# Spreading one row of a table over all SBUF partitions: through DRAM on SyncE's queue, or in one transfer from one partition on GpSimd's queue

## The chip, the cores and the metric

The kernel runs on one core of one Trainium2 chip. The metric is the device time of one execution in microseconds. TensorE (PE) multiplies matrices, VectorE (DVE) and ScalarE (ACT) do elementwise work, GpSimd (POOL) does small copies and issues transfers, and SyncE (SP) issues transfers only. Each engine takes its own list of instructions in order.

## The reference, cut to what matters

```python
def reference(x, w_in, w_out):               # x: 8 x 3008 x 256, d_ff = 2048
    X = np.fft.fft(np.fft.fft(x, axis=1), axis=2).real      # mixing
    t = X.reshape(24064, 256)
    h = np.maximum(t @ w_in, 0.0)
    return h * h @ w_out                     # 24064 x 256
```

The two transforms are matrix products with cosine and sine tables. The real part of the two-dimensional transform is a sum of a cosine product and a sine product. Output rows k and S - k (S = 3008) share both products: one is their sum, the other their difference. The transform over the 256 features is folded into the first weight, so that the first product of the second stage works on the half spectrum, d = 0 to 128.

## The kernel before, in words

The work is cut into 25 windows (`wins`) of up to 512 pairs of output rows; the loop `for w in range(NW)` takes them in order. For every window there are two f16 tiles of 128 partitions, `zc` (cosine part) and `zs` (sine part), four buffers each. They are made ahead: during window w, `z_steps` fills the columns of window w + 1 with matmuls into `pz` (line 536), an ACT copy (line 545) and, for the mirrored columns, a DVE operation on `zs` and `zc` (line 552). These jobs are spread over the steps `lo` to `hi` of a window.

A window has eight steps, `s0` = 0 to 7, each of two chunks of 128 columns of the first weight. In an ordinary step PE multiplies `gh` with `zc` and `zs` into `ph` (lines 804 and 805), ACT takes the relu (line 814), PE turns the sign of the sine part by a third matmul (line 810), and ACT and DVE square both results into `h2` (lines 817 and 819). In the steps that `plan(w)` lists in groups of one or two, the mirrored half is made on DVE instead: PE multiplies the sine part (line 829), ACT copies it times -2 into `sn` (line 837), PE adds the cosine part (line 843), ACT copies it into `hd` (line 845), and DVE adds the two (line 867), takes the relu (line 868) and squares (line 869).

The partition of `zs` that would belong to d = 0 of the sine part is zero in itself and holds the cosine part's row for d = 128 instead. In the mirrored half its sign must not turn, so `sn` has to be corrected: for every chunk a DVE instruction multiplies that row, `eb`, spread over all 128 partitions, by a number per partition, `wv` (line 853, two per step of a group), and another adds it to `sn` (line 857). `row_spread(w)` makes `eb[w]`: it first copies partition 0 of `zs` into a row `zr` in DRAM (line 643), and then reads that row into all 128 partitions (line 645). The second half is kept in the list `row_back` and issued at the head of step 7. `row_spread(w + 1)` is called behind step `hi - 1` of window w (5 in most windows, 6 in some; behind the two steps of a pair where steps go by twos), and only for windows that have groups. `eb` has two buffers. There are 22 such windows.

The second product, `ffn2_steps`, belongs to the window before: PE multiplies `h2` with `wout16` into `po` (line 683), 16 matmuls a piece, ACT copies `po` to `osb` (line 698; three buffers), and `store` issues one or several transfers to the output on SyncE's queue (line 662). These pieces are spread over the eight steps of the next window, so the SyncE list holds stores and the row's two transfers in the order of the program.

For each of the eight batches DVE folds the input (`fold_steps`): `fe`, `fo`, `ab`, `od` and `ev` on lines 392 to 422, with the last value of `od` out of a small matmul (line 418). GpSimd's list holds the loads of `x` (lines 133 and 138, some of them by row indices), the store of `ev` to a DRAM scratch `scr` (line 424), its loads back into `rb` (lines 432 and 434), and four small copies per batch (lines 464 to 466).

Of the kernel before, what the change touches and what calls it, by code (L numbers as in the profile page):

```python
# [9 lines left out]
F16 = mybir.dt.float16  # L10
# [5 lines left out]
P = 128  # L16
# [12 lines left out]
def kernel(  # L29
# [14 lines left out]
    nc = tc.nc  # L44
# [10 lines left out]
    WN = 512  # L55
# [61 lines left out]
    drp = ctx.enter_context(tc.tile_pool(name="drp", bufs=2, space=bass.MemoryType.DRAM))  # L117
# [392 lines left out]
    def zwin(w):  # L510
        if w not in zc:
            zc[w] = zp.tile([P, WN], F16, name="zc", tag="zc")
            zs[w] = zp.tile([P, WN], F16, name="zs", tag="zs")
        return zc[w], zs[w]
# [67 lines left out]
    def run(*jobs):  # L582
        for j in jobs:
            j()
# [48 lines left out]
        nc.vector.tensor_scalar(out=wv, in0=pv[:, 0:NFC], scalar1=2.0, scalar2=None, op0=ALU.mult)  # L633

    eb = {}
    row_back = []

    def row_spread(w):

        wn = wins[w][1]  # L640
        t = eb[w] = tmp.tile([P, WN], F16, name="eb", tag="kf")
        zr = drp.tile([1, WN], F16, name="zr", tag="zr")
        nc.sync.dma_start(out=zr[0:1, 0:wn], in_=zwin(w)[1][0:1, 0:wn])
        src = zr[0:1, 0:wn]
        row_back.append(lambda: nc.sync.dma_start(out=t[:, 0:wn], in_=bass.AP(tensor=src.tensor, offset=src.offset, ap=[[0, P], [1, wn]])))

    def store(osb, p0, g0, m, minus, eng=nc.sync):

# [79 lines left out]
    NST = NFC // 2  # L728
# [16 lines left out]
    def halved(w):  # L745

        return plan(w)[0]
# [4 lines left out]
    for w in range(NW):  # L752
        g0, wn = wins[w]
# [46 lines left out]
        def pq(s):  # L800
            ph = phs[s] = ps_h.tile([P, 2, 512], F32, name="ph", tag="psh")
            for a in range(2):
                f0 = (2 * s + a) * P
                nc.tensor.matmul(ph[:, a, 0:wn], gh[:, 0, f0 : f0 + P], zcw[:, 0:wn], start=True, stop=False)  # L804
                nc.tensor.matmul(ph[:, a, 0:wn], gh[:, 1, f0 : f0 + P], zsw[:, 0:wn], start=False, stop=True)  # L805

        def turn(s):
            for a in range(2):
                f0 = (2 * s + a) * P
                nc.tensor.matmul(phs[s][:, a, 0:wn], gh[:, 2, f0 : f0 + P], zsw[:, 0:wn], start=False, stop=True, skip_group_check=True)  # L810

        def square(s, sg):
            h1 = h1p.tile([P, 2, 512], F16, name="h1", tag="h1")
            nc.scalar.activation(h1[:, :, 0:wn], phs[s][:, :, 0:wn], AF.Relu)  # L814
            hv = rev_dim(h1[:, :, 0:wn], 2) if sg else h1[:, :, 0:wn]
            if sg == 0 and s in by_act:
                nc.scalar.activation(h2[:, 2 * s : 2 * s + 2, 0:wn], hv, AF.Square)  # L817
                return []
            return [lambda: nc.vector.tensor_tensor(h2[:, 2 * s : 2 * s + 2, sg * wn : (sg + 1) * wn], hv, hv, op=ALU.mult)]  # L819
# [5 lines left out]
        def half_q(s):  # L825
            ph = phs[s] = ps_h.tile([P, 2, 512], F32, name="ph", tag="psh")
            for a in range(2):
                f0 = (2 * s + a) * P
                nc.tensor.matmul(ph[:, a, 0:wn], gh[:, 1, f0 : f0 + P], zsw[:, 0:wn], start=True, stop=True)  # L829
            g = two[s]  # L830
            if s == g[0]:
                i = ROT[0] % 2
                ROT[0] += 1
                sns[g] = const.tile([P, 2 * len(g), WN], F16, name=f"sn{i}", tag=f"w16_{i}")
                hds[g] = tmp.tile([P, 2 * len(g), 2 * WN], F16, name="hd", tag="tt")
            i = 2 * g.index(s)
            nc.scalar.activation(sns[g][:, i : i + 2, 0:wn], ph[:, :, 0:wn], AF.Copy, bias=0.0, scale=-2.0)  # L837

        def half_p(s):
            ph, g = phs[s], two[s]  # L840
            for a in range(2):
                f0 = (2 * s + a) * P
                nc.tensor.matmul(ph[:, a, 0:wn], gh[:, 0, f0 : f0 + P], zcw[:, 0:wn], start=False, stop=True, skip_group_check=True)  # L843
            i = 2 * g.index(s)
            nc.scalar.activation(hds[g][:, i : i + 2, 0:wn], ph[:, :, 0:wn], AF.Copy, bias=0.0, scale=1.0)  # L845

        def row_sum(s):

            g = two[s]
            sn, hd = sns[g][:, :, 0:wn], hds[g][:, :, wn : 2 * wn]  # L850

            def row(a):
                nc.vector.tensor_scalar(out=hd[:, a, :], in0=eb[w][:, 0:wn], scalar1=wv[:, 2 * g[0] + a : 2 * g[0] + a + 1], scalar2=None, op0=ALU.mult)  # L853

            if s < g[-1]:
                return []
            return [lambda a=a: row(a) for a in range(2 * len(g))] + [lambda: nc.vector.tensor_tensor(sn, sn, hd, op=ALU.add)]  # L857

        def halves(s):

            if s not in two or s != two[s][-1]:
                return []
            g = two[s]
            sn, hd = sns[g], hds[g]
            hv = hd[:, :, 0 : 2 * wn]
            return [
                lambda: nc.vector.tensor_tensor(rev_dim(hd[:, :, wn : 2 * wn], 2), hd[:, :, 0:wn], sn[:, :, 0:wn], op=ALU.add),  # L867
                lambda: nc.vector.tensor_scalar(out=hv, in0=hv, scalar1=0.0, scalar2=None, op0=ALU.max),  # L868
                lambda: nc.vector.tensor_tensor(h2[:, 2 * g[0] : 2 * g[-1] + 2, 0 : 2 * wn], hv, hv, op=ALU.mult),  # L869
            ]  # L870

        def others(s):
            for j in at[s]:
                j()
            for j in spread(f2, s, NST):
                j()
            for j in post[s]:
                j()
            if s == lo:
                zl[:] = [j for zu, part, h in zj for j in zu(part, h)]  # L880
            if s >= lo:
                for j in spread(zl, s - lo, hi - lo) if s < hi else []:
                    j()
# [44 lines left out]
        for s0 in range(0, NST, ng):  # L928
            ss = range(s0, s0 + ng)
            left = halves(s0 - 1)  # L930
            if s0 == NST - 1:
                while row_back:
                    row_back.pop()()
            if s0 in two and ng == 2:
                for s in ss:
                    half_q(s)
                others(s0)
                run(*row_sum(s0 + 1))
                for s in ss:
                    half_p(s)  # L940
                others(s0 + 1)
                continue
            if s0 in two:
                half_q(s0)
                rows = row_sum(s0)
                run(*(left[0:1] + rows[0:1] + left[1:2] + rows[1:-1] + left[2:3] + rows[-1:]))
                others(s0)
                half_p(s0)
                if s0 == hi - 1 and w + 1 < NW and halved(w + 1):
                    row_spread(w + 1)  # L950
                continue
            for s in ss:
                pq(s)
            for s in ss:
                run(*(left[0:2] + square(s, 0) + left[2:3]))
                left = []
            others(s0)
            for s in ss:
                turn(s)
            for s in ss:  # L960
                run(*square(s, 1))
            if s0 == hi - 1 and ng == 1 and w + 1 < NW and halved(w + 1):
                row_spread(w + 1)
            for s in ss[1:]:
                others(s)
            if s0 < hi <= s0 + ng - 1 and w + 1 < NW and halved(w + 1):
                row_spread(w + 1)
        while row_back:
            row_back.pop()()
        old = (w, h2)  # L970
    for j in ffn2_steps(*old, tail=True):
        j()
# [30 lines left out]
```

## Time and profile before

| | |
|---|---|
| median of 3 runs | 604.29 us (603.27 to 604.42) |
| the profiled execution, its own time | 603.7 us |
| its span, first to last instruction | 601.7 us |
| granted TensorE clock | 0.999 |
| busy: PE, weight loads, DVE, ACT, GpSimd | 579.0, 420.0, 512.5, 514.1, 84.3 us |
| chain of work that ended last | PE 59%, DVE 17%, ACT 10%, DMA 5%, SyncE 1% of the span |

The profile is of one execution. A line of the groups or of a timeline gives the source line, the engine, the operation, the tile written and the tiles read, the shape, and the busy time; the idle time in front of an instruction is named with what ended it. A busy PE is not a PE at its peak, since its matmuls are pipelined and their ends modelled. Idle time of an engine that no other waits for costs nothing.

### The profile page before, as it was taken

The numbers are of one execution on the slowest core, as the hardware profiler recorded it, in microseconds if no ns is written. First come the engines' busy times: TensorE is split into PE (matmuls) and PEld (weight loads), VectorE is DVE, ScalarE is ACT, GpSimd is POOL, SyncE is SP. The second block draws the span as 40 slices with busy tenths as digits, with TensorE's granted clock in tenths as the row PEclk, the third lists the DMA queues.
The fourth block names the chain that finished last, engine by engine and source line by source line (L and its number), as shares of the span: only waits on it lengthen the run. The fifth ranks groups of instructions, "written<-read, shape, count | busy, mean of one in ns | idle before, by whom it ended". The sixth has DMA issues, their size and how long they took to land.

```text
span 601.7 us, 11384 instructions
## 1 busy us (share of the span) xinstructions
PE 579.0 (96%) x4376; PEld 420.0 (70%) x4376; DVE 512.5 (85%) x747; ACT 514.1 (85%) x661; POOL 84.3 (14%) x130
## 2 busy tenths in 40 slices
PE   5899999999999999999999999999999899999997
PEld 2557776776777677777777777777677676776786
DVE  7897578887999987989889899887996899889981
ACT  7687787889999889989999898988989788888972
POOL 6360201102002032020011200411000110000000
PEclk9999999999999999999999999999999999999999
DMA  8955311273224524441164212633112231121222
GB/s 146 203 111 134 90 41 44 46 155 96 64 51 88 135 89 93 107 127 46 53 123 108 87 47 55 113 87 111 49 32 74 69 93 36 46 59 45 64 59 68
DMA packets 39737, 50.33 MB, mean 84 GB/s; under 512 B 4589, under 2 KB 33539, under 8 KB 39683
## 3 DMA queue, kind: packets, MB, share of 16 engines
q0 software_dynamic: 9344, 22.14, 18.3%
q1 hardware_dynamic: 30111, 27.26, 16.0%
q8 instruction: 34, 0.56, 0.4%
q10 hardware_dynamic: 228, 0.21, 0.1%
q14 instruction: 20, 0.16, 0.1%
HBM read 36.42 MB, written 27.86 MB: 107 GB/s over the span
## 4 chain that ended last, share of the span: by engine, by line
PE 59%; DVE 17%; ACT 10%; issue 6%; DMA 5%; SPq 1%; POOL 0%; DVEq 0%; ACTq 0%; POOLq 0%
PE po L683 35%; PE ph L843 5%; PE ph L810 4%; PE ph L829 4%; PE ph L804 4%; PE ph L805 4%; DVE h L869 3%; ACT h L814 3%; PE pz L536 3%; DVE hd L868 2%; DVE hd L867 2%; ACT sn L837 2%; DVE sn L857 2%; DMA zr<-zs 2%; DVE h L819 2%
## 5 line engine op out<-in xcount | busy, mean ns | idle before, releaser
L683 PE MATMUL po<-wout,h 128*128 128x256 f16 (+1 forms) x3024 | 362.2, 273 | 1.8 <-DVE h L869 1.8
L683 PEld LDWEIGHTS <-h 128*128 128x128 f16 (+1 forms) x3024 | 296.3, 98 | 73.9 <-DVE h L869 2.7
L814 ACT ACTIVATE h<-ph 128x1024 f16<-128x1024 f32 (+3 forms) x196 | 185.6, 981 | 14.1 <-PE ph L810 11.1
L845 ACT ACTIVATE hd<-ph 128x1024 f16<-128x1024 f32 (+3 forms) x94 | 94.0, 1001 | 15.1 <-PE ph L843 13.1
L869 DVE TENSOR_TENSOR h<-hd 128x4096 f16<-128x4096 f16 (+6 forms) x51 | 105.4, 2066 | 1.4
L819 DVE TENSOR_TENSOR h<-h 128x1024 f16<-128x1024 f16 (+3 forms) x135 | 85.3, 656 | 21.8 <-ACT h L814 19.7
L837 ACT ACTIVATE sn<-ph 128x1024 f16<-128x1024 f32 (+3 forms) x94 | 93.6, 997 | 0.7 <-PE ph L829 0.7
L698 ACT ACTIVATE osb<-po 128x512 f32<-128x512 f32 (+3 forms) x95 | 54.6, 578 | 24.6 <-PE po L683 23.8
L804 PE MATMUL ph<-zc,gh 128*128 128x512 f16 (+3 forms) x196 | 72.1, 368 | 0.5 <-ACT h L900 0.3
L857 DVE TENSOR_TENSOR sn<-sn,hd 128x2048 f16<-128x2048 f16 (+6 forms) x51 | 56.8, 1114 | 18.5 <-ACT sn L837 15.1
L805 PE MATMUL ph<-zs,gh 128*128 128x512 f16 (+3 forms) x196 | 72.1, 368 | 0.0
L867 DVE TENSOR_TENSOR hd<-hd,sn 128x2048 f16<-128x2048 f16 (+6 forms) x51 | 56.6, 1110 | 11.6 <-ACT hd L845 9.4
L853 DVE TENSOR_SCALAR hd<-eb,wv 128x512 f16<-128x512 f16 (+3 forms) x188 | 53.7, 345 | 13.3 <-DMA eb<-zr 13.3
L817 ACT ACTIVATE h<-h 128x1024 f16<-128x1024 f16 (+3 forms) x61 | 62.7, 1028 | 1.9
L868 DVE TENSOR_SCALAR hd<-hd 128x4096 f16<-128x4096 f16 (+6 forms) x51 | 56.8, 1113 | 1.6
L843 PE MATMUL ph<-zc,gh 128*128 128x512 f16 (+3 forms) x188 | 54.6, 372 | 3.4 <-ACT sn L837 2.5
L810 PE MATMUL ph<-zs,gh 128*128 128x512 f16 (+3 forms) x196 | 55.3, 368 | 0.3 <-ACT h L814 0.2
L829 PE MATMUL ph<-zs,gh 128*128 128x512 f16 (+3 forms) x188 | 54.5, 372 | 0.0
L805 PEld LDWEIGHTS <-gh 128*128 128x128 f16 x196 | 19.1, 98 | 21.1 <-issue 1.0
L804 PEld LDWEIGHTS <-gh 128*128 128x128 f16 x196 | 19.1, 97 | 20.3
L829 PEld LDWEIGHTS <-gh 128*128 128x128 f16 x188 | 18.3, 97 | 20.9
L843 PEld LDWEIGHTS <-gh 128*128 128x128 f16 x188 | 17.1, 97 | 11.1 <-issue 6.8
(144 smaller groups left out, 398.6 us busy)
## 6 DMA issues: line engine op xcount, KB each, us to landing
out_dram<-osb SPq DMA_DIRECT2D x77, 128.0 KB
xo<-in_x_dram POOLq DMA_DIRECT2D x7, 768.0 KB
scr<-ev POOLq DMA_DIRECT2D x8, 390.0 KB, 3.1
eb<-zr SPq DMA_DIRECT2D x19, 128.0 KB
rb<-scr POOLq DMA_DIRECT2D x16, 130.0 KB
out_dram<-osb SPq DMA_DIRECT2D x12, 94.0 KB
w<-in_moe_w_in_dram POOLq DMA_DIRECT2D x2, 512.0 KB
wout<-in_moe_w_out_dram POOLq DMA_DIRECT2D x1, 1024.0 KB
```

What stands on the lines that cost most here:

```text
L683: nc.tensor.matmul(po[0:m, j * D : (j + 1) * D], h2[:, fc, q : q + m], wout16[:, fc, :], start=(fc == 0 and (j == 0 or not four or i > 3)) ...
L804: nc.tensor.matmul(ph[:, a, 0:wn], gh[:, 0, f0 : f0 + P], zcw[:, 0:wn], start=True, stop=False)
L805: nc.tensor.matmul(ph[:, a, 0:wn], gh[:, 1, f0 : f0 + P], zsw[:, 0:wn], start=False, stop=True)
L810: nc.tensor.matmul(phs[s][:, a, 0:wn], gh[:, 2, f0 : f0 + P], zsw[:, 0:wn], start=False, stop=True, skip_group_check=True)
L814: nc.scalar.activation(h1[:, :, 0:wn], phs[s][:, :, 0:wn], AF.Relu)
L819: return [lambda: nc.vector.tensor_tensor(h2[:, 2 * s : 2 * s + 2, sg * wn : (sg + 1) * wn], hv, hv, op=ALU.mult)]
L829: nc.tensor.matmul(ph[:, a, 0:wn], gh[:, 1, f0 : f0 + P], zsw[:, 0:wn], start=True, stop=True)
L837: nc.scalar.activation(sns[g][:, i : i + 2, 0:wn], ph[:, :, 0:wn], AF.Copy, bias=0.0, scale=-2.0)
L843: nc.tensor.matmul(ph[:, a, 0:wn], gh[:, 0, f0 : f0 + P], zcw[:, 0:wn], start=False, stop=True, skip_group_check=True)
L845: nc.scalar.activation(hds[g][:, i : i + 2, 0:wn], ph[:, :, 0:wn], AF.Copy, bias=0.0, scale=1.0)
L857: return [lambda a=a: row(a) for a in range(2 * len(g))] + [lambda: nc.vector.tensor_tensor(sn, sn, hd, op=ALU.add)]
L869: lambda: nc.vector.tensor_tensor(h2[:, 2 * g[0] : 2 * g[-1] + 2, 0 : 2 * wn], hv, hv, op=ALU.mult),
```

## The change

The row goes from partition 0 of `zs` to all 128 partitions of `eb` in one transfer. Its source is read with a step of 0 over the 128 partitions of the target, 1 KB each in a full window (the window's columns times 2 bytes). It is issued on GpSimd's queue where `row_spread` is called, so it stands in GpSimd's list between what the steps up to there and the later ones issue. The copy `zr` in DRAM, the two transfers on SyncE's queue, the list `row_back` and both places that empty it are gone. The places of the calls of `row_spread` stay.

```diff
     eb = {}
-    row_back = []
 
     def row_spread(w):
 
         wn = wins[w][1]
         t = eb[w] = tmp.tile([P, WN], F16, name="eb", tag="kf")
-        zr = drp.tile([1, WN], F16, name="zr", tag="zr")
-        nc.sync.dma_start(out=zr[0:1, 0:wn], in_=zwin(w)[1][0:1, 0:wn])
-        src = zr[0:1, 0:wn]
-        row_back.append(lambda: nc.sync.dma_start(out=t[:, 0:wn], in_=bass.AP(tensor=src.tensor, offset=src.offset, ap=[[0, P], [1, wn]])))
+        row = zwin(w)[1][0:1, 0:wn]
+        nc.gpsimd.dma_start(out=t[:, 0:wn], in_=bass.AP(tensor=row.tensor, offset=row.offset, ap=[[row.ap[0][0], 1], [0, P], [1, wn]]))
...
             left = halves(s0 - 1)
-            if s0 == NST - 1:
-                while row_back:
-                    row_back.pop()()
             if s0 in two and ng == 2:
...
                 row_spread(w + 1)
-        while row_back:
-            row_back.pop()()
         old = (w, h2)
```

## The prediction

> **What bounds the kernel now.** I read the page first, then the waits, then the chain of work that ended last, then single engines in the stretches that the chain points to. The page puts TensorE (PE) at 579.0 us of 601.7, VectorE (DVE) at 512.5 and ScalarE (ACT) at 514.1. PE has 18.2 us of gaps when I add up those over 50 ns, 10.0 of them before 50 us, where nothing of this change happens. So the change can win back only PE gaps that hang on the row.
>
> The waits, by engine and line (who waited for whom, us in total, times, longest):
>
> ```profile
> DVE hd L853 <- DMA eb<-zr: 13.3, 4, 5.1
> PE pz L536 <- DVE od L418: 2.1, 1, 2.1
> PE po L683 <- DVE h L869: 1.8, 3, 0.8
> ```
>
> DVE stands four times for the spread row. No PE instruction waits for L853 itself, but PE waits for DVE work queued behind it. The SyncE queue's own waits show where the row's time goes:
>
> ```profile
> SPq L662 <- ACT osb L698: 297.3, 72, 38.8
> ...
> SPq L645 <- DMA zr<-zs: 67.4, 21, 6.3
> ```
>
> SyncE takes its list in order: the row waits behind output stores (L662) whose tiles are not copied yet, then for its own trip to DRAM. The chain (start, us, what) between 395 and 480 us:
>
> ```profile
> 399.25 6.51 DMA zr<-zs
> ...
> 405.81 3.60 DMA eb<-zr
> ...
> 448.92 5.43 DMA zr<-zs
> ...
> 454.40 3.12 DMA eb<-zr
> ...
> 475.12 0.11 DVE od L418
> ```
>
> And the timelines of DVE and PE (start, busy, what, in brackets the idle time before it and its releaser):
>
> ```profile
> 409.44 1.14 DVE L853 TENSOR_SCALAR hd<-eb,wv 128x512 f16<-128x512 f16 x4 [4.93 <-DMA eb<-zr]
> ...
> 457.55 1.14 DVE L853 TENSOR_SCALAR hd<-eb,wv 128x512 f16<-128x512 f16 x4 [5.14 <-DMA eb<-zr]
> ```
> ```profile
> 424.78 0.94 PE L683 MATMUL po<-wout,h 128*128 128x256 f16 x7 [0.70 <-DVE h L869]
> ...
> 475.27 0.49 PE L536 MATMUL pz<-sin,od 128*128 128x376 f16 x2 [2.12 <-DVE od L418]
> ...
> 503.58 0.61 PE L683 MATMUL po<-wout,h 128*128 128x256 f16 x4 [0.36 <-DVE h L869]
> ```
>
> From 457.55 on DVE works without a pause to the od at 475.04, which PE awaits: the late row costs PE 2.12 us. The row at 409.44 is followed in the same way by the 0.70 us gap at 424.78, and by 0.10 us at 418.93 (behind ACT). The other two late rows, at 122.00 (2.41 us) and 526.35 (0.83), cost nothing: behind the first PE has no gap until 149.4, behind the second DVE waits for ACT anyway (0.99 and 0.90 us).
>
> **What the change removes.** 44 issues on SyncE (22 of L643, 22 of L645), 0.25 and 0.35 us each, and the wait in between. Output stores queued behind them start earlier; that is worth nothing, because no ACT copy into osb (L698) waits for a store: its idle time is put down to PE alone (23.8 us). The row no longer stands behind stores. PE, ACT and DVE keep every instruction in its order.
>
> **What it adds.** 22 issues on GpSimd (POOL), each placed behind step 5's other work. Price of one issue: 0.55 us (L432, two in 1.1) to 2.74 us (the longest L138); near 0.6, as the direct L424. From issue to landing no row shows this transfer (one partition read 128 times). The bound below is eb<-zr from DRAM, the same 128 packets of 1 KB to the same tile, 3.1 to 3.6 us in the chain; rb<-scr,idx_r, 130 KB on GpSimd's own queue, takes 4.2. The bound above: the 128 packets leave the one partition one after the other. Queue q1 moved 30111 packets in 16.0% of 16 engines' 601.7 us, 51 ns each, so 6.5 us, behind the 3.1 us that scr<-ev needs on this queue: 9.6 us. I take 4.2, the nearest row in queue and bytes.
>
> The page "SBUF — State Buffer" of the Trainium skill, section "Door 1: the DMA port swizzle", speaks against the change: partitions 0 to 3 share one port, measured at 27.6 GB/s. By it 131 KB take an estimated 4.7 us before start and completion, between my two bounds, and the sum below comes out the same. No row of this trace reads one partition in bulk.
>
> **When each transfer can start.** POOL runs its list in order but waits for data alone, so it issues at the later of two moments: its previous instruction is done, and the row of zs is written. Rows that show this:
>
> ```profile
> 387.20 2.74 POOL L138 DMA_INDIRECT xo<-in_x_dram,idx_r  x1 [0.30 <-issue]
> ...
> 439.84 0.33 POOL L466 COPY spn<-yt 128x2 f16<-128x2 f16 x1
> ...
> 514.31 0.33 POOL L466 COPY spn<-yt 128x2 f16<-128x2 f16 x1
> ```
> ```profile
> 487.35 0.55 ACT L545 ACTIVATE zs<-pz 128x121 f16<-128x121 f32 x2 [0.40 <-PE pz L536]
> ```
>
> For the row used at 409.4, POOL is free at 389.9 (zs is there at 389.1) and DVE comes for it at 404.5: 14.6 us of slack. For 457.5: free at 440.2, needed at 452.4, 12.2 us. For 526.3: 514.6 to 525.5, 10.9. For 122.0: zs at 111.9, needed at 119.6, 7.7. Done for all 22 rows, the shortest slacks are 6.1 us (69.6 to 75.7, the first row), 7.7, 8.2 (487.9 to 496.1), 10.9, 11.4 (225.7 to 237.1) and 12.2; the other 16 have 13 or more. With 4.2 us all four waits go. With 9.6 us three rows are late: the first by 3.5, where DVE is busy 5.1 of 10 us and PE waits for nothing of its; the one at 122.0 by 1.9, less than the 2.4 that cost nothing before; and the one at 496.1 by 1.4. There DVE runs without a pause to the 0.36 us gap at 503.58, so this costs PE 1.4 one for one.
>
> **What queues behind the new wait.** On POOL behind the rows: the scratch store L424, the rb loads L432 and L434, the x loads, the small copies L464 to L466. In the present order each of them waits for a later DVE or DMA event than the row does, except L464 at 152.33 and 225.30, pushed about 1 us; the copies behind those (L465) start at 161.1 and 230.2, so this costs nothing. In the queue the transfer may stand behind x gathers (8.9 us to land) at 318.5 and 389.9: 8.9 + 4.2 leads to 331.6 and 403.0, needed at 332.9 and 404.5. Does POOL's issuing slow DVE? Of 23 L853 that ran beside a POOL DMA issue, two were longer than the usual 348 ns (402 and 486): nothing.
>
> **The sum.** PE wins 2.12 + 0.70 + 0.10 = 2.92 us. After it, od is earlier by up to 5.1 us against PE's 2.1, so it is not late next; next are the 0.36 at 503.58 and 0.79 at 550.92, which stay. The profiled execution has a span of 601.7 and took 603.7; it becomes 598.8 and 600.8. It lies 0.6 under the median of 604.29, which becomes **601.4**.
>
> **Rivals.**
> - *Slower: the one-partition read.* If it takes over about 11 us to land, the row at 496.1 is late by 2.9 and the gain is gone. At 14 us that row is late by 5.8 one for one; those with slack 10.9 and 12.2 are late by 3.1 and 1.8, of which PE felt 2.92 of 10.07 before (29%), 1.4: 7.2 - 2.9 = +4.3, 608.6. For it: no row of this pattern. Against: even strictly one packet after the other it is 9.6. Chance 0.14.
> - *The issue starves.* DVE is busy 9.7 of 10 us from 490 to 500, and POOL's L138 took 0.98 us at best, 2.74 at worst. If an issue is held through a stretch of 8 us, the row of 487.9 lands at 500.1, 4.0 late, one for one: 604.29 - 2.9 + 4.0 = 605.4. Against: the longest hold seen is 1.8 us. Chance 0.08. The same page's box "The 'DVE blocks DMA' trap (SWDGE)" gives the reason: DMAs issued from GpSimd are held out while DVE is in a two-port mode; the spread of L138 agrees in direction.
> - *No gain.* The rows come in time, but ACT, busy 8.7 to 9.4 of 10 us from 400 to 470, takes DVE's place and PE waits there: 604.3. Against: PE's largest gap behind ACT from 400 to 510 us is 0.26. Chance 0.12.
> - *Part of it.* One of the two gaps stays, 0.8 to 2.1 us won: 602.2 to 603.5. Chance 0.14.
>
> **How the numbers follow.** The forecast has 0.52, its own range 600.4 to 602.4. A measurement of this kernel tells 0.2% from no change, 1.2 us: faster is under 603.1. Faster: 0.52 and 0.12 of the part and 0.02 of the rest, 0.66. Within: 0.02, 0.10 and 0.08, 0.20. Slower: 0.14. The range reaches from 600.0 over the cases without gain and with starved issues to 605.5 and leaves the slow case out.
>
> **What would show it.** Right: the wait of L853 for the eb transfer under 3 us in total; L536 at about 473 us without a gap of 2 us; SyncE without waits for zr; POOL with 22 more issues of about 0.6 us, one near 390. Wrong: L853 waiting at many windows (the read is slow), issues of several us on POOL (starved), or a new PE gap behind ACT between 400 and 480 us.

## The result, and the profile after

The changed kernel takes 600.71 us (median of 5 runs, 600.49 to 600.90) against 604.29 before (5 runs, 603.27 to 604.75): ratio 0.9945, 95% interval 0.993 to 0.996. The profiled execution took 600.49 us with a span of 598.7, 3.0 us less than before.

The waits of the changed kernel (who waited for whom, us in total, times, longest; L850 is the old L853, L642 the new issue):

```profile
DVE hd L850 <- DMA eb<-zs: 0.4, 1, 0.4
POOL eb L642 <- ACT zs L545: 61.8, 8, 22.2
POOL eb L642 <- DVE zs L552: 51.8, 4, 22.9
ACT osb L695 <- PE po L680: 23.8, 57, 1.2
```

DVE waits 0.4 us for rows where it waited 13.3. In 12 of the 22 issues GpSimd waits for the row of `zs` itself, that is, it stands ready before there is anything to send. SyncE's own waits hold no row any more, only stores. The timelines of DVE and PE at the places that answer to those shown of before:

```profile
404.37 1.14 DVE L850 TENSOR_SCALAR hd<-eb,wv 128x512 f16<-128x512 f16 x4
...
451.42 1.13 DVE L850 TENSOR_SCALAR hd<-eb,wv 128x512 f16<-128x512 f16 x4
```
```profile
472.08 0.48 PE L536 MATMUL pz<-sin,od 128*128 128x376 f16 x2
...
500.38 1.70 PE L680 MATMUL po<-wout,h 128*128 128x256 f16 x14 [0.36 <-DVE h L866]
```

Neither row has a bracket (no idle time before it): DVE takes the rows without a pause, 5.1 and 6.1 us earlier than before. The matmul on `od` has lost its 2.12 us gap and starts 3.2 us earlier. The 0.36 us gap has stayed and is 3.2 us earlier too. GpSimd's timeline shows the early starts:

```profile
387.15 2.73 POOL L138 DMA_INDIRECT xo<-in_x_dram,idx_r  x1 [0.30 <-issue]
389.88 0.61 POOL L642 DMA_DIRECT2D eb<-zs  x1
...
437.96 0.66 POOL L642 DMA_DIRECT2D eb<-zs  x1
```

They were 399.25 and 448.92 on SyncE. The price of the new source stands in the first row, issued at 69.79 and awaited until 76.08, and in the queue table (packets, MB, share of 16 engines):

```profile
q0 software_dynamic: 10400, 24.94, 32.0%
q1 hardware_dynamic: 26899, 24.44, 13.6%
```

GpSimd's queue, q0, had 18.3% before. The 13.7% more are 0.137 x 16 x 598.7 = 1312 us of engine time for 22 rows, 3.7 us on all 16 engines for each; SyncE's queue gave back 2.4% for the two transfers.

### The profile page after: what moved, and what is told of

Its sections match the earlier page's. It is cut to its first block, busy times and chain, and to the rows that moved or that the text cites. A ratio compares the mean times of both kernels' runs of the same rounds, so it can differ in the third digit from the quotient of the medians.

```text
span 598.7 us, 11343 instructions
## 1 busy us (share of the span) xinstructions
PE 579.3 (97%) x4376; PEld 420.6 (70%) x4376; DVE 512.9 (86%) x747; ACT 514.0 (86%) x661; POOL 96.7 (16%) x152
## 4 chain that ended last, share of the span: by engine, by line
PE 67%; DVE 12%; ACT 12%; issue 7%; DMA 1%; POOL 0%; ACTq 0%; DVEq 0%; SPq 0%; POOLq 0%
PE po L680 40%; PE ph L840 5%; PE ph L807 5%; PE ph L801 5%; PE ph L802 5%; PE ph L826 5%; ACT h L811 3%; PE pz L536 3%; ACT sn L834 3%; ACT osb L695 2%; DVE h L866 2%; ACT hd L842 2%; DVE hd L865 2%; DVE hd L864 2%; DVE sn L854 1%
## 5 line engine op out<-in xcount | busy, mean ns | idle before, releaser
L842 ACT ACTIVATE hd<-ph 128x1024 f16<-128x1024 f32 (+3 forms) x94 | 94.0, 1001 | 14.7 <-PE ph L840 13.3
L850 DVE TENSOR_SCALAR hd<-eb,wv 128x512 f16<-128x512 f16 (+3 forms) x188 | 53.9, 345 | 0.4 <-DMA eb<-zs 0.4
L802 PEld LDWEIGHTS <-gh 128*128 128x128 f16 x196 | 19.1, 98 | 21.2 <-issue 1.0
L801 PEld LDWEIGHTS <-gh 128*128 128x128 f16 x196 | 19.1, 97 | 20.3
L826 PEld LDWEIGHTS <-gh 128*128 128x128 f16 x188 | 18.3, 97 | 20.9
L642 POOL DMA_DIRECT2D eb<-zs x22 | 13.2, 601 | 120.0 <-ACT zs L545 61.8
```

## The experiments

Each was run beside the kernel before on the same chip; ratios are against that. The kernel before has a median of 606.0 us beside the first two kernels below and the two that ask which rows win, 605.09 beside the one on ScalarE's queue, beside itself once more and beside the two with extra transfers, and 604.95 beside the last four. Its executions fall in two groups by granted clock, 603.8 to 605.4 us at 0.998 and over and 605.5 to 606.8 at 0.997 and under, so ratios of a percent's fraction depend on how many of each there were. Where that matters I compare "at equal clock": only executions at 0.998 and over, where the kernel before has medians of 604.56, 604.57 and 604.78 us.

**Which part wins: the queue or the missing copy in DRAM?**

The row through DRAM, both transfers on GpSimd's queue (the changed kernel's place):

```diff
-        row = zwin(w)[1][0:1, 0:wn]
-        nc.gpsimd.dma_start(out=t[:, 0:wn], in_=...row, step 0 over P...)
+        zr = drp.tile([1, WN], F16, name="zr", tag="zr")
+        nc.gpsimd.dma_start(out=zr[0:1, 0:wn], in_=zwin(w)[1][0:1, 0:wn])
+        src = zr[0:1, 0:wn]
+        nc.gpsimd.dma_start(out=t[:, 0:wn], in_=bass.AP(tensor=src.tensor, offset=src.offset, ap=[[0, P], [1, wn]]))
```

> The row still goes through DRAM, but both transfers are issued on GpSimd's queue where the change issues its one. Theory (the gain comes from the earlier start, on a queue without output stores): the row starts at 389.9 and 438 us as in the changed kernel and lands some 7 to 8 us later (two trips), within the slack of all rows but the shortest; 600.7 us, within 0.6. Rival (the gain comes from leaving out the trip through DRAM): no gain, 604.3 us, and VectorE waits for the row again.

Measured: 600.69 us (ratio 0.9921, 0.9904 to 0.9937); DVE waits for no row. The copy in DRAM costs nothing here: the whole gain, 3.9 us at equal clock, is had without leaving it out. In the trace the packets of the second transfer end 2.9 to 5.5 us after its issue, those of the changed kernel's one transfer 5.6 to 8.5 (9.6 and 10.5 right behind loads of x).

The one transfer on SyncE's queue:

```diff
-        nc.gpsimd.dma_start(out=t[:, 0:wn], in_=...row...)
+        nc.sync.dma_start(out=t[:, 0:wn], in_=...row...)
```

> One transfer from one partition, without the DRAM copy, but on SyncE's queue. Theory (the start matters): the row starts behind the output stores as before, near 399 and 449 us, and lands about 6 us later, so it is late at 457.5 by about 2.5 us instead of 5.1, at 409.4 by about 1 instead of 4.9, and newly late near 496 by up to 1.9; 601.5 to 603.5 us. Rival (the trip through DRAM is what cost time): 600.7 us as in the changed kernel.

Measured: 602.25 us (0.9943, 0.9927 to 0.996). Its waits and PE timeline:

```profile
DVE hd L850 <- DMA eb<-zs: 10.4, 3, 4.3
```
```profile
426.12 1.27 PE L680 MATMUL po<-wout,h 128*128 128x256 f16 x10 [0.30 <-DVE h L866]
...
475.77 0.49 PE L536 MATMUL pz<-sin,od 128*128 128x376 f16 x2 [1.28 <-DVE od L418]
```

Three rows are still late, the two that matter by 4.2 and 4.3 us where 1 and 2.5 were expected (4.9 and 5.1 before), none near 496; both gaps are there, smaller (0.30 and 1.28 us for 0.70 and 2.12). One trip for two, alone, wins 2.5 us at equal clock (602.11 us); the early start, alone, won all 3.9 in the kernel above. This kernel and the one before read the row of 376 columns on the same queue, in packets of 752 B that no other transfer has: from one partition a packet takes 340 ns at the median and the last ends 5.0 us after the issue, from DRAM 36 ns and 2.8 us. For the row of 448 columns (896 B) the difference is smaller, 404 ns and 5.6 us for 192 ns and 4.8 us.

The one transfer on ScalarE's queue:

```diff
-        nc.gpsimd.dma_start(out=t[:, 0:wn], in_=...row...)
+        nc.scalar.dma_start(out=t[:, 0:wn], in_=...row...)
```

> The one transfer issued on ScalarE's queue at the same place. Theory (any queue without output stores will do): the row starts right behind the copies of zs and 600.5 to 601.5 us is reached, unless ScalarE, in order and busy 9 of 10 us, stands for the columns that VectorE writes, which could cost up to 2 us. Rival (GpSimd's queue itself is what helps): 603 us or more with L850 waiting for the row as before.

Measured: 601.08 us (0.9937, 0.9922 to 0.9951), and 0.6 us of waiting for one row. A queue without output stores is what counts, not GpSimd's.

**Which rows win?**

```diff
     def row_spread(w):
...
+        if w in (17, 19):          # the second kernel: w not in (17, 19)
+            (the one transfer on GpSimd's queue)
+            return
         (the two transfers on SyncE's queue, as before)
```

> The change is made for the rows of windows 17 and 19 alone (used at 409.4 and 457.5 us before); the other 20 rows go through DRAM on SyncE's queue as before. Theory (all of the gain hangs on these two rows): 600.7 to 601.3 us, with the PE gaps near 424.8 (0.70) and 475.3 (2.12) gone. Rival (the gain is spread over all rows, or comes from relief of SyncE's queue): 2 of 22 of it, 0.3 us, 604.0 us.

> The change is made for all rows but those of windows 17 and 19. Theory: the two PE gaps of 0.70 and 2.12 us stay, 603.5 to 604.5 us. Rival (the gain is spread over all rows): 20 of 22 of it, 601.0 us.

Measured: the two rows alone 600.85 us (0.9924, 0.9908 to 0.994), all but them 604.10 us (0.998, 0.9967 to 0.9992). In the second kernel PE has gaps that answer to those of before:

```profile
419.88 0.59 PE L814 MATMUL ph<-zs,gh 128*128 128x512 f16 x2 [1.16 <-ACT h L818]
425.74 1.26 PE L687 MATMUL po<-wout,h 128*128 128x256 f16 x10 [0.70 <-DVE h L873]
```

and 1.85 us in front of the matmul on `od` at 475.95, together 3.71. The ratio of the second kernel leaves 1 out by a little, because more executions of the kernel before ran at the lower clock (10 of 17, for 2 of 12). At equal clock the two rows alone win 3.7 us, where all rows through DRAM on GpSimd's queue won 3.9, and the other 20 rows win 0.6. Of these 0.6, 0.2 lie outside the span from first to last instruction (2.0 us in the kernel before, 1.8 here); no PE gap in the profiles accounts for the rest, and it is of the size of the scatter. So two of 22 rows carry nearly all of the gain, and relief of SyncE's queue by the other 20 brings little or nothing.

**The kernel before, once more**, with no edit but a blank line:

> The kernel before, once more (a blank line moved), for a second profile: on the chip of the first four runs its times spread from 603.8 to 606.8, while the kernels with early rows stayed within 0.7. Theory: the spread comes from how late the rows are, so in this profile PE's gaps beyond the usual ones stand behind L853's waits for the row, and grow with the time: 604 to 606.5 us. Rival: the spread is of the chip and shows in gaps elsewhere, the same in both kernels.

Measured: 605.52 us (603.86 to 606.76), the profiled execution 606.76. Its row waits are 14.0 us for 13.3, and the three gaps are 0.77, 0.70 and 2.16 us, 3.63 for 2.92. That is a part of the difference. The larger part, 2.4 us, is there at 70 us already, before any row is used. The stretch of 10 to 20 us in this profile and in that of before (us, then PE, weight loads, DVE, ACT, GpSimd busy, granted clock, DMA share, GB/s):

```profile
10.00:20.00 10.00, 7.27 (x34) 3.34 (x34) 7.30 (x15) 4.74 (x11) 5.55 (x9) 0.83 1.18 190
```
```profile
10.00:20.00 10.00, 7.55 (x45) 3.92 (x45) 8.57 (x16) 5.78 (x14) 5.50 (x10) 1.00 1.18 189
```

The granted clock is 0.83 there for 1.00. PE's timelines at that place, in this profile and in that of before:

```profile
15.27 0.65 PE L536 MATMUL pz<-cos,od 128*128 128x376 f16 x3 [2.19 <-DVE od L408]
```
```profile
14.64 0.65 PE L536 MATMUL pz<-cos,od 128*128 128x376 f16 x3 [1.55 <-DVE od L408]
```

PE first waits 0.6 us longer for an early `od`, and then runs at half the clock for 3.4 us, from 16.4 to 19.8 us, which costs 1.6 us more. My theory was right for 0.7 us of 3.0. The rest lies elsewhere, as the rival said, but it isn't the same in all kernels, as the last section shows.

**What does a slow transfer cost?** One or two more transfers of the same row, to tiles that nobody reads, queued ahead of the real one:

```diff
     eb = {}
+    dum = [const.tile([P, WN], F16, name=f"dum{i}") for i in range(1)]     # range(2) in the second kernel
...
+        for o in dum:
+            nc.gpsimd.dma_start(out=o[:, 0:wn], in_=...row, step 0 over P...)
         nc.gpsimd.dma_start(out=t[:, 0:wn], in_=...row, step 0 over P...)
```

> The changed kernel with one more transfer of the same row from the same partition, to a tile that nobody reads, queued ahead of each real one; landing goes from about 6.4 to about 12 us after issue. The slower rival of the prediction, now with its price measured: the row used at 492.9 us (8.2 us of slack) comes 3 to 4 us late and costs PE that one for one, the rows with 10.8 and 11.4 us of slack about 1 us that costs little; 603.5 to 605 us. Other theory (a few late us of VectorE are absorbed there too): 600.7 to 602 us.

> As the kernel with one extra transfer, but two of them, landing about 17 us after issue: nearly all rows are late, by 2 to 10 us, 80 us in all; the one at 492.9 costs PE 9 one for one, the others 29% of what VectorE stands, as the late rows did before, 10 to 15 us: 612 to 625 us. Other theory (absorbed): under 606 us.

Measured: 635.82 us (1.0504, 1.047 to 1.0538) and 710.86 us (1.175, 1.1713 to 1.1787). Both expectations are far off: the first kernel lost 35 us where 3 to 4 were expected. Its waits say why:

```profile
ACT osb L698 <- DMA out_dram<-osb: 32.8, 9, 8.1
DVE hd L853 <- DMA eb<-zs: 9.0, 3, 3.3
```

DVE waits less for rows than in the kernel before. But ACT now waits for output stores to leave the `osb` buffers, which it never did, and PE waits behind ACT. The worst of it, on ACT and on PE:

```profile
581.46 0.60 ACT L698 ACTIVATE osb<-po 128x512 f32<-128x512 f32 x1 [8.11 <-DMA out_dram<-osb]
```
```profile
583.94 1.01 PE L843 MATMUL ph<-zc,gh 128*128 128x512 f16 x2 [7.77 <-ACT sn L837]
```

PE's gaps over 50 ns sum to 40.1 us for 14.7 in the changed kernel; 25 of the 31 us between the spans are these. The mean granted clock of the profiled execution fell from 1.0 to 0.988, which is of the size of the rest (0.012 x 579 = 7 us). With two extra transfers the waits for stores are 74.2 us and those for rows 69.0, so there both count. Two further kernels test this reading on the kernel with one.

A fourth buffer for `osb` in the kernel with one extra transfer, and in another the extra transfer read from all partitions:

```diff
-    osp = ctx.enter_context(tc.tile_pool(name="osp", bufs=3))
+    osp = ctx.enter_context(tc.tile_pool(name="osp", bufs=4))
```
```diff
-            nc.gpsimd.dma_start(out=o[:, 0:wn], in_=...row, step 0 over P...)
+            nc.gpsimd.dma_start(out=o[:, 0:wn], in_=zwin(w)[1][:, 0:wn])
```

> The kernel with one extra transfer, and a fourth buffer for osb. With three, ScalarE stood 32.8 us (9 times, 8.1 at most) for an output store to leave its buffer. Theory (reads from one partition hold the output stores back, and the stores hold ScalarE and so PE): the fourth buffer gives some 6 us more, these waits all but go, 603 to 612 us, and what stays is VectorE's 9 us for late rows. Rival (late rows, or the load on the transfer engines as such): 630 us or more again.

> The extra transfer reads the whole tile of zs, 128 partitions to 128 partitions, instead of one partition 128 times: as many bytes, packets and issues. Theory (one partition is what is slow): it adds well under 2 us to the row's landing, no store holds ScalarE, 600.5 to 602 us. Rival (22 more transfers of 128 KB are what costs): 630 us or more.

Measured: 609.38 us with the fourth buffer (1.0063, 1.0038 to 1.0089) and 601.64 us with the extra transfer read from all partitions (0.9935, 0.9913 to 0.9956). ACT's waits for stores, in this order:

```profile
ACT osb L698 <- DMA out_dram<-osb: 11.5, 4, 3.9
```
```profile
ACT osb L698 <- DMA out_dram<-osb: 3.2, 2, 2.5
```

With the fourth buffer DVE still waits 8.8 us for rows, for 9.0 without it, so a buffer that has nothing to do with the row gives 26 of the 35 us back. Read from all partitions, the same bytes cost about 1 us instead of 35. It is the read from one partition that holds the stores.

How near is the changed kernel to that point? It, and the one with the row through DRAM on GpSimd's queue, with two `osb` buffers:

```diff
-    osp = ctx.enter_context(tc.tile_pool(name="osp", bufs=3))
+    osp = ctx.enter_context(tc.tile_pool(name="osp", bufs=2))
```

> The changed kernel with two osb buffers instead of three: how near is it to the point where its one-partition read holds the stores? ACT copies two apart are 8 to 9 us from each other in most places, a store is issued within 2 us and lands in 2 to 4, held back by up to 5 us behind a row's read: 601 to 605 us, with waits of L695 for stores. If the stores have room to spare: 600.7 us.

> The row through DRAM on GpSimd's queue, with two osb buffers. Theory (the trip through DRAM holds the stores less than the read from one partition): less wait for stores and 1 to 4 us faster than the changed kernel with two buffers, 600.7 to 602.5 us. Rival: both the same.

Measured: 624.57 us (1.031, 1.0286 to 1.0335) and 608.69 us (1.0058, 1.0037 to 1.008). In the changed kernel with two buffers:

```profile
ACT osb L695 <- DMA out_dram<-osb: 22.0, 7, 6.5
```

And with the row through DRAM:

```profile
ACT osb L697 <- DMA out_dram<-osb: 9.0, 4, 3.7
```

Both lose more than expected, and the difference, 16 us, is four times what I had thought at most: the one-partition read holds the stores already in the changed kernel, and the third buffer covers it. The kernel before was not run with two buffers, so how much of the 8 us that the version through DRAM loses is due to its row is open. Of the versions tried, the row through DRAM on GpSimd's queue is as fast as the changed kernel and further from that point.

## Why the prediction was right, and where it was not

- *The step that carried the forecast* held: the gaps of 0.10, 0.70 and 2.12 us are gone (2.92), and 0.36 and 0.79 stayed. One new gap of 0.14 us stands behind ACT at 427.61. Span forecast 598.8, measured 598.7; that the small remainders cancel to 0.1 is luck. That these gaps hang on the two rows is shown by the kernel with only those two changed. The median fell by 3.58, which is 0.7 more than the sum. Of that, 0.2 lies outside the span (603.7 - 601.7 = 2.0 us before, 600.49 - 598.7 = 1.8 after), where the sum did not look. Some 0.4 more is there because the profiled execution lay 0.6 us under the median before and only 0.2 under it after. What the other executions lost there is open: the same gaps can be larger, 3.63 us in the second profile of the kernel before, but executions without a profile can't be read in this way.
- *When each transfer can start*: 389.9 and 440.2 were forecast, 389.88 and 437.96 measured. The second is early because the DVE work that GpSimd's copies ahead of it wait for (the last `yt`, line 458) starts 2.1 us earlier, at 436.69 for 438.83: DVE had won more than PE there, and the forecast kept DVE's times as they were. The shortest slack, 6.1 us, was the one used up: the first row landed 0.4 us late at 76.08 and cost PE nothing.
- *The price of one issue*: 538 to 696 ns in all 22, near the 0.6 taken. No issue was held up, so the rival of the starving issue did not occur; the box of the Trainium skill's page "SBUF — State Buffer" that spoke for it ("The 'DVE blocks DMA' trap (SWDGE)") finds nothing in these 22. The indirect loads of line 138 still take up to 2.73 us to issue, as the row above shows, so the runs say nothing against it for these.
- *The price from issue to landing was mis-sized*: I took 4.2 us, the row nearest in queue and bytes, between ends of 3.1 and 9.6. Measured are 6.3 for the first row and 5.6 to 8.5 for those with no loads of x ahead. The source decided, not the queue. The first row's packets, told apart by their size, end 5.0 us after the issue on SyncE's queue, 5.6 on ScalarE's and 5.9 on GpSimd's; from DRAM they end after 2.8 on SyncE's and 3.0 on GpSimd's. For the row of 448 columns it is 5.6 on all three, and from DRAM 4.8 and 3.4. The slack covered it, so the sum did not notice.
- *The rule that spoke against the change was right in size.* In the kernel with one extra transfer, two rows (262 KB) run, in most windows, from about 1.2 to 11.3 us after the first issue, 26 GB/s. The Trainium skill, "SBUF — State Buffer", section "Door 1: the DMA port swizzle", gives 27.6 GB/s for partitions 0 to 3; the trace agrees within a tenth. Had I taken the estimate of 4.7 us that I worked out from this figure, behind the 1.16 us that the first packet needs, the landing would have come out at an estimated 5.9.
- *The slower rival had the wrong mechanism.* It put the price of a slow transfer on late rows, 4 us at 14 us of landing. In the kernel with one extra transfer the row lands some 11 us after its own issue at the median, and the kernel loses 35 us, most of it without any wait for a row. What failed is the step on the removed issues, where the output stores were "worth nothing": I looked at ACT's wait for stores in the profile of before, found none, and priced the stores at nothing; I did not ask what the new transfer does to the stores that run beside it, nor how far three buffers reach.
- *No gain* and *part of it* did not occur: PE has no gap behind ACT over 0.26 us from 400 to 500 us.

## What to carry to other kernels

Look for the queue before the path: a small transfer that stands in order behind stores starts when the stores may, and moving its issue to a list with nothing late in it won all there was, with or without the trip through DRAM. Count only the waits behind which the bounding engine stands: 2 of 22 rows carried nearly all of the gain. A transfer that reads one partition many times costs the others beside it, so look at how many buffers of slack those have before it is doubled; the profile shows no wait until the last buffer is used up.

## What the runs showed of the hardware that I had not expected

- One partition read 128 times holds its packets two to ten times as long as a row in DRAM does (340 and 36 ns for 752 B, 404 and 192 ns for 896 B), and it delays output stores, which read up to 128 partitions: 35 us for one more of them per window, 1 us for the same bytes from 128 partitions. Which part of the path is shared (the partition's port, or the transfer engines' queues behind it) these runs don't separate. The traces have one hint: the stores' own packets of 1 KB don't get longer. Their median is 46 ns while a row is read and at other times, in the changed kernel and in the one with an extra transfer. So the delay lies between packets, which speaks for the transfer engines but doesn't show it.
- Where PE stands long, the granted clock often drops to half for 3.4 us or a multiple. In the changed kernel with two `osb` buffers this begins at 207.4, 415.6, 466.8 and 558.9 us, in or up to 1 us behind PE gaps of 5.69, 3.83, 2.59 and 2.05 us. Not every such gap has it: in the kernel with one extra transfer those of 3.71 us at 213.8 and 3.35 us at 279.2 have none. The mean clock was 0.984 with 31 us of gaps, 0.988 with 40 and 0.943 with 94.
- In 28 of 60 executions of the kernel before the mean granted clock was 0.997 or less, and where one was profiled the clock was 0.83 between 10 and 20 us, long before the first row. The one transfer on SyncE's queue shows the same dip in its profile. In these two profiles PE's wait for the early `od` at 13 us is the longest of all 14, 2.19 and 1.89 us for 1.22 to 1.79. The four kernels whose two late rows start early on a queue without stores (the changed one, and those through DRAM on GpSimd's queue, on ScalarE's, and with two rows only) show 0.998 or more in all 23 executions; the kernel with all rows but two has the lower clock in 2 of 12. Why a change that acts at 390 us should go with the clock at 16 us is open.
